# DCN-v2 cross layers: a block transpose on VectorE, x0's rows in eight loads, and one sum on GpSimd

## The chip, the cores and the metric

The kernel runs on one core of a Trainium2 chip. The metric is device time in microseconds (us) of one execution; lower is better. The core has TensorE (matrix multiply, PE in the profile, its weight loads PEld), VectorE (DVE), ScalarE (ACT), GpSimd (POOL) and SyncE (SP, which here only issues transfers). Each engine works through its own list of instructions in order and waits for others on semaphores. A transfer (DMA) is issued by an instruction in some engine's list: SPq and ACTq are the rows of those issues.

## What is computed

Six cross layers over a batch of 4096 rows of 416 features, all in bfloat16:

```python
B, F, D, L = 4096, 26, 16, 6
Din = min(F * D, 1024)            # 416
def reference(x0, ws, bs):        # x0 (B, Din), ws (L, Din, Din), bs (L, Din)
    x = x0
    for l in range(ws.shape[0]):
        x = x0 * (x @ ws[l] + bs[l]) + x
    return x
```

## The kernel before

**Layout.** Layers 0 to 4 keep x transposed: features on partitions, batch along the row. The 416 features are three blocks of 128 (`XM`, index m or k) and a remainder of 32 (`XR`). The batch is two halves s = 0, 1 of 2048 (`SW`), each of four groups g of 512 columns (`CW`). The remainder of a half is folded: partitions 32g to 32g+31 of `XR` hold the 32 remainder features of group g, so that a half is one 128x512 tile. `XRd` is the same with its upper and lower 64 partitions exchanged; the first layer uses it for m = 1 (line 218).

**Loads.** SP issues, in this order: the transposing loads of x0 into `XM[0]` (`load_x0t`, line 75; two groups interleaved with ScalarE's issues, then the rest), after the fifth of them `xrem` (the 32 remainder features of the second half, line 84), three more transposing loads, the weights of layer 1 (line 71), the remainder rows of the weights `WR` (line 90), the weights of layers 2 to 5, x0 by rows `X0rows` in four loads of eight 128-row blocks (line 123), and the last layer's bias `bLr` (line 125). ScalarE issues the weights of layer 0, the biases, the first half's remainder `xrig[:, 0]` in four loads (line 80) and `WR` of layer 0, and then copies that `WR` to two other partition groups (line 108), GpSimd to a third (line 110). An issue waits first for the previous transfer that used the same one of eight transfer semaphores.

**The remainder of x0.** It has to be transposed. `x0_rem(s, tpr)` (line 153) does it on TensorE: four 128x128 transposes of `xrig` into PSUM, then three VectorE copies out of PSUM, one to `XR[0]` and two of 64 partitions, exchanged, to `XRd`. For the first half it stands in the middle of the first six matmul groups of layer 0; for the second half it stands after the first half's remainder matmuls (`mm_rem`), in the other half of the PSUM tile `pr` (line 255). For the second half GpSimd first rearranges `xrem` into `xrig[:, 1]` (line 132).

**Layer 0** (`first_layer`) works on a half as two times 1024 columns (h), for each m a PSUM tile `ph`. PSUM holds four such tiles. `ew_main` evicts a tile: ScalarE adds the bias (line 163), VectorE multiplies by x0 (line 164) and adds x (line 167). `ew_rem` does the same for the folded remainder (lines 171 to 173). Layers 1 to 4 run through the same steps, with `mm_full`, `mm_row` and `mm_rem`.

**The last layer** turns the product round, so that the batch rows come out on partitions: the transposed x is the stationary operand and the weights stream (lines 325, 331, 334; the bias enters by a matmul with ones). x itself is transposed back into `XLrows` by transposing transfers. The 32 blocks of 128 rows are done in four rounds of eight. A block's PSUM result is cast by ScalarE into `t` (line 352), multiplied by `X0rows` on VectorE (line 353), and `XLrows` is added on VectorE (line 342); then the result `o` is stored. A sum is put off by one: `ew` emits the product of a block and then `close_sum` emits the sum of the block before it, with its store. The first rounds handle two blocks in one instruction (832 elements), the last round, from q = 6, eight single blocks u = 0 to 7 (416 elements). Stores are issued by SP, that of the very last block by ScalarE (line 367).

The order of instructions on each engine is made by a scheduler when the program is built; `tc.keep_in_program_order` fixes an instruction's place relative to the others fixed on the same engine. Each tile pool gives out a fixed number of buffers in turn: six `t`, ten `o`, four PSUM tiles.

Of the kernel before, what the change touches and what calls it, by code (L numbers as in the profile page):

```python
# [10 lines left out]
ALU = mybir.AluOpType  # L11
BF16 = mybir.dt.bfloat16
# [4 lines left out]
def kernel(  # L17
# [7 lines left out]
    nc = tc.nc  # L25
    B, D = x0.shape
    L = ws.shape[0]
    P = 128
    NK = 3
    R = D - NK * P  # L30
    assert R == 32 and B == 4096 and D == 416 and L >= 2
    NS = 2
    NG = 4
    CW = 512
    SW = NG * CW
# [4 lines left out]
    big = ctx.enter_context(tc.tile_pool(name="big", bufs=1))  # L40
# [4 lines left out]
    x0_v = x0.rearrange("(bt p) d -> p bt d", p=P)  # L45
    out_v = out.rearrange("(bt p) d -> p bt d", p=P)

    ident = const.tile([P, P], BF16)
# [9 lines left out]
    X0rows = big.tile([P, NBT, D], BF16)  # L58
    XLrows = big.tile([P, NBT, D], BF16)
    scrR = [big.tile([P, 4, P], BF16, name=f"scrR{s}") for s in range(NS)]  # L60
    xrem = big.tile([P, 16, R], BF16)
    xrig = big.tile([P, NS, 4, P], BF16)
    XRd = big.tile([P, NS * CW], BF16)
    XM = [big.tile([P, NK, B], BF16, name=f"XM{i}") for i in range(3)]
    XR = [big.tile([P, NS * CW], BF16, name=f"XR{i}") for i in range(3)]

    def col0(s, g):
        return SW * s + CW * g

    def load_wm(eng, l):  # L70
        eng.dma_start(WM[:, l], ws[l, 0:NK * P, :].rearrange("(k p) n -> p k n", p=P))

    def load_x0t(s, g):
        c0 = col0(s, g)
        nc.sync.dma_start_transpose(out=XM[0][:, :, c0:c0 + CW], in_=x0[c0:c0 + CW, 0:NK * P])

    def load_xrem0():
        with nc.allow_non_contiguous_dma(reason="64B row segments"):
            for i in range(4):
                nc.scalar.dma_start(xrig[:, 0, i, :].rearrange("p (g r) -> p g r", g=NG), x0_v[:, i:16:4, NK * P:D])  # L80

    def load_xrem1():
        with nc.allow_non_contiguous_dma(reason="64B row segments"):
            nc.sync.dma_start(xrem[:], x0_v[:, 16:32, NK * P:D])

    def load_wr0():
        nc.scalar.dma_start(WR[0:R, 0, :], ws[0, NK * P:D, :])
# [17 lines left out]
    for g in range(1, NG):  # L105
        dst, src = WR[32 * g:32 * g + 32, 0, :], WR[0:R, 0, :]
# [4 lines left out]
    for g in range(2, NG):  # L111
        load_x0t(0, g)
    load_x0t(1, 0)
    load_xrem1()
    for g in range(1, NG):
        load_x0t(1, g)
    load_wm(nc.sync, 1)
# [1 line left out]
        load_wr(nc.sync, g, 1, L)  # L119
    for l in range(2, L):  # L120
        load_wm(nc.sync, l)
    for q in range(4):
        nc.sync.dma_start(X0rows[:, 8 * q:8 * q + 8, :], x0_v[:, 8 * q:8 * q + 8, :])
    for g in range(NG):
        nc.sync.dma_start(bLr[32 * g:32 * g + 1, :], bs[LL:LL + 1, :])

    def fill_wd(l0, l1):
        for g in range(NG):
            nc.gpsimd.tensor_copy(WD[32 * g:32 * g + 32, l0:l1, g, :], WR[32 * g:32 * g + 32, l0:l1, NK * P:D])

    fill_wd(0, 1)
    nc.gpsimd.tensor_copy(xrig[:, 1].rearrange("p i (g r) -> p i g r", g=NG), xrem[:].rearrange("p (g i) r -> p i g r", g=NG))
    fill_wd(1, L)

    wps = psum.tile([P, CW], FP32, tag="ps", name="wps")
# [14 lines left out]
        nc.vector.tensor_copy(bM[:], pb[:, 0:NK, 0:L])  # L150
        nc.vector.tensor_copy(bR[:], pb[:, 3, 0:L])

    def x0_rem(s, tpr):
        for i in range(4):
            nc.tensor.transpose(tpr[:, 128 * i:128 * i + 128], xrig[:, s, i, :], ident[:])  # L155
        for dst, src in ((slice(0, P), slice(0, P)), (slice(64, P), slice(0, 64)), (slice(0, 64), slice(64, P))):
            to = XR[0] if dst == src else XRd
            nc.vector.tensor_copy(to[dst, CW * s:CW * s + CW], tpr[src])

    def ew_main(l, s, m, h, pt, cur, nxt, pin=False):  # L160
        c0 = col0(s, 2 * h)
        t = tpool.tile([P, 2 * CW], BF16, name="t")
        nc.scalar.activation(t[:], pt[:].rearrange("p a b -> p (a b)"), ACT.Identity, bias=bM[:, m, l:l + 1], scale=1.0)  # L163
        prod = nc.vector.tensor_tensor(out=t[:], in0=t[:], in1=XM[0][:, m, c0:c0 + 2 * CW], op=ALU.mult)  # L164
        if pin:
            tc.keep_in_program_order(prod)
        nc.vector.tensor_tensor(out=nxt[:, m, c0:c0 + 2 * CW], in0=t[:], in1=cur[:, m, c0:c0 + 2 * CW], op=ALU.add)  # L167
# [38 lines left out]
    def first_layer(s):  # L206
        cur, curR, nxt, nxtR = XM[0], XR[0], XM[1], XR[1]

        def full(pt, m, h, gl, after_row):
            c0 = col0(s, 2 * h + gl)  # L210
            for k in range(NK):
                nc.tensor.matmul(pt[:, gl, :], lhsT=WM[:, 0, k, 128 * m:128 * m + 128], rhs=cur[:, k, c0:c0 + CW],  # L212
                                 start=(k == 0 and not after_row), stop=(k == NK - 1 and after_row))

        def row(pt, m, h, opens):
            for gl in range(2):
                rg = 32 * ((2 * h + gl) ^ (2 if m == 1 else 0))
                src = XRd if m == 1 else curR
                nc.tensor.matmul(pt[:, gl, :], lhsT=WR[rg:rg + 32, 0, 128 * m:128 * m + 128],  # L219
                                 rhs=src[rg:rg + 32, CW * s:CW * s + CW],  # L220
                                 start=opens, stop=not opens, tile_position=(rg, 0))

        def ph(m):
            return psum.tile([P, 2, CW], FP32, tag="ps", name=f"ph{m}")

        pa = [ph(m) for m in range(NK)]
        if s == 0:
            for m in range(NK):
                full(pa[m], m, 0, 0, False)
            tp0 = psum.tile([P, CW], BF16, tag="ps", name="tpr")  # L230
            x0_rem(0, tp0[:])
            for m in range(NK):
                full(pa[m], m, 0, 1, False)
        else:
            for m in range(NK):
                for gl in range(2):
                    full(pa[m], m, 0, gl, False)
        pb = [ph(0)]
        row(pa[0], 0, 0, False)
        row(pb[0], 0, 1, True)  # L240
        row(pa[2], 2, 0, False)
        row(pa[1], 1, 0, False)
        for m in range(NK):
            ew_main(0, s, m, 0, pa[m], cur, nxt)
        for m in range(NK):
            if m:
                pb.append(ph(m))
            for gl in range(2):
                full(pb[m], m, 1, gl, m == 0)
        row(pb[1], 1, 1, False)  # L250
        row(pb[2], 2, 1, False)
        pr = psum.tile([P, 2, CW], FP32, tag="ps", name="pr")
        mm_rem(0, s, pr[:, 0, :], cur, curR)
        if s == 0:
            x0_rem(1, pr[:, 1, :].bitcast(BF16)[:, 0:CW])
        for m in range(NK):
            ew_main(0, s, m, 1, pb[m], cur, nxt, pin=(s == 0))
        ew_rem(0, s, pr[:, 0, :], curR, nxtR)
# [3 lines left out]
    for s in range(NS):  # L262
        first_layer(s)
# [16 lines left out]
    for l in range(1, LL):  # L280
        nxt, nxtR = XM[1 + (l % 2)], XR[1 + (l % 2)]
        feeds_last = (l == LL - 1)
        tiles = [(s, m) for s in range(NS) for m in range(NK)]
# [31 lines left out]
    NQ = len(quads)  # L315
# [7 lines left out]
    def mm_q_full(q, g, py, closes):  # L323
        for k in range(NK):
            nc.tensor.matmul(py[:, 0:D], lhsT=cur[:, k, q_cols(q, g)], rhs=WM[:, l, k, :],  # L325
                             start=((not closes) and k == 0), stop=(closes and k == NK - 1))
# [8 lines left out]
                             rhs=bLr[32 * g:32 * g + 1, :], start=False, stop=(g < done), tile_position=(32 * g, 0))  # L335

    pending = []

    def close_sum():
        while pending:  # L340
            o, t, xl, dst, eng = pending.pop()
            tc.keep_in_program_order(nc.vector.tensor_tensor(out=o, in0=t, in1=xl, op=ALU.add))  # L342
            eng.dma_start(dst, o)

    def ew(q, g0, n, src, eng):
        s, i = quads[q]
        b0 = 16 * s + 4 * g0 + i
        b = slice(b0, b0 + 4 * (n - 1) + 1, 4)
        t = tpool.tile([P, 2 * CW], BF16, name="t")
        o = opool.tile([P, 2, D], BF16, name="o")  # L350
        tv = t[:, 0:n * D].rearrange("p (a d) -> p a d", a=n)
        nc.scalar.copy(tv, src)  # L352
        tc.keep_in_program_order(nc.vector.tensor_tensor(out=tv, in0=tv, in1=X0rows[:, b, :], op=ALU.mult))  # L353
        close_sum()
        pending.append((o[:, 0:n, :], tv, XLrows[:, b, :], out_v[:, b, :], eng))

    PAIRS = [(0, 0), (0, 1), (1, 0), (1, 1), (2, 0), (2, 1), (3, 0), (3, 1)]
# [3 lines left out]
    for q, at, done in rounds:  # L361
        tiles = [psum.tile([P, 2, CW], FP32, tag="ps", name=f"py{n}") for n in range(4)]
        bank = [tiles[n][:, a, :] for n, a in at]

        def close(u, n):
            tl, a = at[u]
            ew(q + u // 4, u % 4, n, tiles[tl][:, a:a + n, 0:D], nc.scalar if q + 2 == NQ and u == 7 else nc.sync)

        for u in range(done):
            mm_q_full(q, u, bank[u], False)  # L370
        mm_q_rem(q, bank[0:4], done)
        close(0, done)
        mm_q_rem(q + 1, bank[4:8], 0)
        for u in range(done, 8):
            mm_q_full(q + u // 4, u % 4, bank[u], True)
            if at is not PAIRS:
                close(u, 1)
            elif u % 2:
                close(u - 1, 2)
    close_sum()  # L380


# [28 lines left out]
```

## Time and profile before

| what | value |
|---|---|
| runs | 130.68, 130.64, 130.82 us (median 130.68) |
| profiled execution | 130.58 us, of which the span of its instructions is 128.8 |
| TensorE busy | 123.6 us (96% of the span), 1691 matmuls |
| VectorE busy | 106.7 us (83%), 195 instructions |
| ScalarE busy | 86.9 us (67%), 99 instructions |
| GpSimd busy | 6.2 us (5%), 18 instructions |
| transfers | 16.37 MB; the 16 transfer engines nearly always busy up to about 39 us |
| TensorE clock granted | full in every slice of the span |

Times in the views are from the start of the span. A timeline row has start, duration, engine, line, operation, output and inputs, shapes and, after x, how many instructions it merges. A row of the groups of instructions has, after the count, the busy time in us and the mean of one in ns, then the idle time just before them and what ended it. A row of the chain of waits has start, duration, engine, tile and line.

### The profile page before, as it was taken

What the parts mean: (1) busy time and instruction counts of PE and PEld (TensorE: products, weight loads), DVE (VectorE), ACT (ScalarE), POOL (GpSimd) and SP (SyncE); (2) the same over time, 40 slices, a digit from 0 to 9 for tenths busy, and PEclk for the clock granted to TensorE, in tenths of its full rate; (3) what the DMA queues carried; (4) which work ended last, traced back from release to release, by engine and by line L of the source; (5) the groups of instructions that cost most, each with busy time, mean ns of one, the idle gap of its engine ahead of it and who ended that gap; (6) DMA issues with size and microseconds to landing.
All of it is one profiled execution on the core that took longest, in us unless ns stands there. A gap on an engine that the chain in (4) does not pass through costs nothing.

```text
span 128.8 us, 3973 instructions
## 1 busy us (share of the span) xinstructions
PE 123.6 (96%) x1691; PEld 55.1 (43%) x1691; DVE 106.7 (83%) x195; ACT 86.9 (67%) x99; POOL 6.2 (5%) x18
## 2 busy tenths in 40 slices
PE   7999999999999999999999999999999999999960
PEld 3343443344545444434444544444444445445420
DVE  0023989999999898989898989898989899898991
ACT  0138873887848667848668848668858896569670
POOL 4004300600000000000000000000000000000000
PEclk9999999999999999999999999999999999999999
DMA  4999999999990000000000000000297999985754
GB/s 95 244 231 207 163 153 264 253 328 333 336 291 9 5 0 8 0 0 5 0 5 0 5 0 5 0 5 0 45 163 169 119 237 191 217 261 186 235 178 138
DMA packets 42102, 16.37 MB, mean 127 GB/s; under 512 B 30906, under 2 KB 42084, under 8 KB 42084
## 3 DMA queue, kind: packets, MB, share of 16 engines
q1 hardware_dynamic: 39368, 15.53, 53.9%
q10 hardware_dynamic: 2716, 0.59, 2.5%
q8 instruction: 13, 0.21, 0.7%
q14 instruction: 5, 0.04, 0.1%
HBM read 6.15 MB, written 3.41 MB: 74 GB/s over the span
## 4 chain that ended last, share of the span: by engine, by line
PE 89%; DVE 6%; issue 2%; ACT 1%; DVEq 0%
PE pt L179 49%; PE ph L212 13%; PE py L325 8%; PE pt L185 5%; PE pr L196 5%; PE wps L139 4%; DVE t L353 4%; DVE o L342 2%; PE pr L191 2%; PE ph L219 1%; PE py L331 1%; PE py L334 1%; ACT t L352 1%; PE tpr L155 0%; PE pr L155 0%
## 5 line engine op out<-in xcount | busy, mean ns | idle before, releaser
L179 PE MATMUL pt<-XM,WM 128*32 128x512 bf16 x1152 | 65.2, 379 | 0.0
L163 ACT ACTIVATE t<-pt,bM 128x1024 bf16<-128x1024 f32 x48 | 49.6, 1115 | 18.5 <-PE pt L185 18.5
L164 DVE TENSOR_TENSOR t<-t,XM 128x1024 bf16<-128x1024 bf16 x60 | 41.4, 690 | 5.2 <-ACT t L163 5.2
L167 DVE TENSOR_TENSOR XM<-t,XM 128x1024 bf16<-128x1024 bf16 x60 | 41.8, 697 | 3.4
L179 PEld LDWEIGHTS <-WM 128*32 128x32 bf16 x1152 | 29.7, 97 | 33.8 <-issue 5.1
L352 ACT CAST t<-py 128x416 bf16<-128x416 f32 (+1 forms) x23 | 14.8, 642 | 4.8 <-PE py L325 2.6
L325 PE MATMUL py<-WM,XM 128*128 128x416 bf16 x96 | 17.7, 340 | 0.0
L212 PE MATMUL ph<-XM,WM 128*128 128x512 bf16 x72 | 16.5, 381 | 0.0
L163 ACT ACTIVATE t<-ph,bM 128x1024 bf16<-128x1024 f32 x12 | 12.5, 1114 | 3.4 <-PE ph L219 3.4
L325 PEld LDWEIGHTS <-XM 128*128 128x128 bf16 x96 | 9.0, 98 | 8.5 <-issue 1.4
L353 DVE TENSOR_TENSOR t<-t,X0rows 128x416 bf16<-128x416 bf16 (+1 forms) x23 | 10.4, 457 | 1.2 <-ACT t L352 1.2
L342 DVE TENSOR_TENSOR o<-t,XLrows 128x416 bf16<-128x416 bf16 (+1 forms) x23 | 10.4, 456 | 0.0
L212 PEld LDWEIGHTS <-WM 128*128 128x128 bf16 x72 | 6.7, 98 | 8.4 <-issue 1.1
L171 ACT ACTIVATE t<-pr,bR 128x512 bf16<-128x512 f32 x10 | 6.4, 685 | 2.7 <-PE pr L196 2.1
L196 PE MATMUL pr<-XM,WM 128*32 128x512 bf16 x120 | 8.2, 379 | 0.0
L185 PE MATMUL pt<-XR,WR 32*128 32x512 bf16 x96 | 7.3, 379 | 0.0
L139 PE MATMUL wps<-const-bfloat16-1.0 128*128 128x512 bf16 (+1 forms) x12 | 4.9, 592 | 0.8 <-PEq L395 0.8
L104 ACT ACT_TABLE_LOAD x1 | 1.3, 1283 | 6.0 <-DMA XM<-in_x_dram 6.0
L173 DVE TENSOR_TENSOR XR<-t,XR 128x512 bf16<-128x512 bf16 x10 | 4.2, 425 | 0.7
L196 PEld LDWEIGHTS <-WM 128*32 128x32 bf16 x120 | 3.2, 97 | 3.0
L150 DVE CAST bM<-pb 128x18 f32<-128x18 bf16 x1 | 0.2, 177 | 5.1 <-PE pb L149 5.1
L172 DVE TENSOR_TENSOR t<-t,XR 128x512 bf16<-128x512 bf16 x10 | 4.2, 420 | 0.0
(38 smaller groups left out, 33.5 us busy)
## 6 DMA issues: line engine op xcount, KB each, us to landing
X0rows<-in_x_dram SPq DMA_DIRECT2D x4, 832.0 KB, 11.5
out_dram<-o SPq DMA_DIRECT2D x9, 208.0 KB, 2.5
WM<-in_ws_dram SPq DMA_DIRECT2D x5, 312.0 KB
out_dram<-o SPq DMA_DIRECT2D x13, 104.0 KB, 1.9
WR<-in_ws_dram SPq DMA_DIRECT2D x4, 130.0 KB, 4.1
WM<-in_ws_dram ACTq DMA_DIRECT2D x1, 312.0 KB
XM<-in_x_dram SPq DMA_TRANSPOSE x8, 4.9
xrig<-in_x_dram ACTq DMA_DIRECT2D x4, 32.0 KB, 4.2
```

The costliest lines, as they stand in the source:

```text
L139: nc.tensor.matmul(wps[:, 0:cols], lhsT=warm[:, 0:P], rhs=warm[:, 0:cols], start=True, stop=True)
L163: nc.scalar.activation(t[:], pt[:].rearrange("p a b -> p (a b)"), ACT.Identity, bias=bM[:, m, l:l + 1], scale=1.0)
L164: prod = nc.vector.tensor_tensor(out=t[:], in0=t[:], in1=XM[0][:, m, c0:c0 + 2 * CW], op=ALU.mult)
L167: nc.vector.tensor_tensor(out=nxt[:, m, c0:c0 + 2 * CW], in0=t[:], in1=cur[:, m, c0:c0 + 2 * CW], op=ALU.add)
L179: nc.tensor.matmul(pts[g // 2][32 * q:32 * q + 32, g % 2, :], lhsT=WM[:, l, k, 128 * m + 32 * q:128 * m + 32 * q + 32], rhs=cur[:, k, c0:c ...
L185: nc.tensor.matmul(pts[g // 2][:, g % 2, :], lhsT=WR[32 * g:32 * g + 32, l, 128 * m:128 * m + 128], rhs=curR[32 * g:32 * g + 32, CW * s:CW ...
L196: nc.tensor.matmul(pr[32 * g:32 * g + 32, :], lhsT=WM[:, l, k, NK * P:D], rhs=cur[:, k, c0:c0 + CW], start=False, stop=(k == NK - 1), tile ...
L212: nc.tensor.matmul(pt[:, gl, :], lhsT=WM[:, 0, k, 128 * m:128 * m + 128], rhs=cur[:, k, c0:c0 + CW], start=(k == 0 and not after_row), sto ...
L325: nc.tensor.matmul(py[:, 0:D], lhsT=cur[:, k, q_cols(q, g)], rhs=WM[:, l, k, :], start=((not closes) and k == 0), stop=(closes and k == NK ...
L342: tc.keep_in_program_order(nc.vector.tensor_tensor(out=o, in0=t, in1=xl, op=ALU.add))
L352: nc.scalar.copy(tv, src)
L353: tc.keep_in_program_order(nc.vector.tensor_tensor(out=tv, in0=tv, in1=X0rows[:, b, :], op=ALU.mult))
```

## The change

Three things are changed.

First, the remainder of the second half is no longer transposed by TensorE. `xrem` is loaded in another layout, partition p holding the sixteen batch rows 16p to 16p+15 of the half, by ScalarE and not by SP. The load is made to wait for a one-column memset of `xrem` that VectorE executes after the first half's copies. Then VectorE transposes `xrem` in blocks of 32x32 directly into `XR[0]`, and makes the two exchanged copies to `XRd` from `XR[0]`, in SBUF. The four TensorE transposes, the three copies from PSUM and GpSimd's rearrangement of `xrem` go; `xrig` keeps the first half alone. VectorE's instructions of both halves are now fixed in program order.

Second, `X0rows` is loaded in eight transfers of four blocks for four of eight.

Third, in the last round the sum of block u = 3 is made by GpSimd, fixed in program order, and its store is issued by ScalarE. `close_sum` has one sum less to do.

```diff
-    xrig = big.tile([P, NS, 4, P], BF16)
+    xrig = big.tile([P, 4, P], BF16)
...
+    def pin(ins):
+        tc.keep_in_program_order(ins)
...
     def load_xrem1():
+        pin(nc.vector.memset(xrem[:, 0, 0:1], 0.0))
         with nc.allow_non_contiguous_dma(reason="64B row segments"):
-            nc.sync.dma_start(xrem[:], x0_v[:, 16:32, NK * P:D])
+            pin(nc.scalar.dma_start(xrem[:], x0[SW:2 * SW, NK * P:D].rearrange("(p t) r -> p t r", p=P)))
...
     load_x0t(1, 0)
-    load_xrem1()
     for g in range(1, NG):
...
-    for q in range(4):
-        nc.sync.dma_start(X0rows[:, 8 * q:8 * q + 8, :], x0_v[:, 8 * q:8 * q + 8, :])
+    for q in range(8):
+        nc.sync.dma_start(X0rows[:, 4 * q:4 * q + 4, :], x0_v[:, 4 * q:4 * q + 4, :])
...
     fill_wd(0, 1)
-    nc.gpsimd.tensor_copy(xrig[:, 1].rearrange("p i (g r) -> p i g r", g=NG), xrem[:].rearrange("p (g i) r -> p i g r", g=NG))
     fill_wd(1, L)
...
-    def x0_rem(s, tpr):
+    def x0_rem0(tpr):
         for i in range(4):
-            nc.tensor.transpose(tpr[:, 128 * i:128 * i + 128], xrig[:, s, i, :], ident[:])
+            nc.tensor.transpose(tpr[:, 128 * i:128 * i + 128], xrig[:, i, :], ident[:])
         for dst, src in ((slice(0, P), slice(0, P)), (slice(64, P), slice(0, 64)), (slice(0, 64), slice(64, P))):
             to = XR[0] if dst == src else XRd
-            nc.vector.tensor_copy(to[dst, CW * s:CW * s + CW], tpr[src])
+            pin(nc.vector.tensor_copy(to[dst, 0:CW], tpr[src]))
+        load_xrem1()
+
+    def x0_rem1():
+        pin(nc.vector.transpose(XR[0][:, CW:2 * CW].rearrange("p (j t) -> p t j", t=16), xrem[:]))
+        for dst, src in ((slice(64, P), slice(0, 64)), (slice(0, 64), slice(64, P))):
+            pin(nc.vector.tensor_copy(XRd[dst, CW:2 * CW], XR[0][src, CW:2 * CW]))
...
         if s == 0:
-            x0_rem(1, pr[:, 1, :].bitcast(BF16)[:, 0:CW])
+            x0_rem1()
...
     pending = []
+    late = []
...
-    def ew(q, g0, n, src, eng):
+    def ew(q, g0, n, src, eng, on_pool=False):
...
         close_sum()
+        if on_pool:
+            tc.keep_in_program_order(nc.gpsimd.tensor_tensor(out=o[:, 0:n, :], in0=tv, in1=XLrows[:, b, :], op=ALU.add))
+            late.append((out_v[:, b, :], o[:, 0:n, :]))
+            return
         pending.append((o[:, 0:n, :], tv, XLrows[:, b, :], out_v[:, b, :], eng))
...
-            ew(q + u // 4, u % 4, n, tiles[tl][:, a:a + n, 0:D], nc.scalar if q + 2 == NQ and u == 7 else nc.sync)
+            ew(q + u // 4, u % 4, n, tiles[tl][:, a:a + n, 0:D], nc.scalar if q + 2 == NQ and u == 7 else nc.sync,
+               q + 2 == NQ and u == 3)
...
+    for dst, o in late:
+        nc.scalar.dma_start(dst, o)
     close_sum()
```

In the order that the scheduler builds, the load of `xrem` stands on ScalarE right after the two `WR` copies and before the first eviction; VectorE's block transpose stands where the three copies from PSUM stood, after the first half's first three pairs of product and sum; and ScalarE's store of u = 3 stands between the casts of u = 5 and u = 6, with a wait for GpSimd, although the source has it after the loop.

More of the change, by code (lines that the diff above doesn't have):

```diff
@@ L79, in load_xrem0 @@
             for i in range(4):
-                nc.scalar.dma_start(xrig[:, 0, i, :].rearrange("p (g r) -> p g r", g=NG), x0_v[:, i:16:4, NK * P:D])
+                nc.scalar.dma_start(xrig[:, i, :].rearrange("p (g r) -> p g r", g=NG), x0_v[:, i:16:4, NK * P:D])
     def load_xrem1():
+        pin(nc.vector.memset(xrem[:, 0, 0:1], 0.0))
         with nc.allow_non_contiguous_dma(reason="64B row segments"):
-            nc.sync.dma_start(xrem[:], x0_v[:, 16:32, NK * P:D])
+            pin(nc.scalar.dma_start(xrem[:], x0[SW:2 * SW, NK * P:D].rearrange("(p t) r -> p t r", p=P)))
     def load_wr0():
@@ L230, in first_layer @@
             tp0 = psum.tile([P, CW], BF16, tag="ps", name="tpr")
-            x0_rem(0, tp0[:])
+            x0_rem0(tp0[:])
             for m in range(NK):
```

## The prediction

> **What bounds the kernel now.** I read the chain of waits first, with the page's summary of it, in order of time:
>
> ```profile
> PE 89%; DVE 6%; issue 2%; ACT 1%; DVEq 0%
> 16.06 0.65 PE pr L196 x12
> 16.71 0.33 PE pr L155 x4
> 17.04 3.88 PE ph L212 x18
> ...
> 115.45 0.19 PE py L334 x2
> 115.65 0.02 issue
> 115.67 0.86 ACT t L352
> ...
> 125.24 0.37 DVE t L353
> 125.62 0.29 DVE o L342
> 125.90 0.28 DVEq L406
> ```
>
> TensorE runs without a gap from 0.77 to 115.65 us, so what it no longer executes there is time saved; the four transposes of line 155 for the second half are such a piece, 0.33 us. From 115.67 the chain goes over to ScalarE and VectorE. To see which of them ends the last round I read the timeline around 123 us, VectorE and then ScalarE:
>
> ```profile
> 122.97 0.37 DVE L353 TENSOR_TENSOR t<-t,X0rows 128x416 bf16<-128x416 bf16 x1
> 123.25 0.37 DVE L342 TENSOR_TENSOR o<-t,XLrows 128x416 bf16<-128x416 bf16 x1
> ...
> 125.24 0.37 DVE L353 TENSOR_TENSOR t<-t,X0rows 128x416 bf16<-128x416 bf16 x1
> 125.53 0.66 DVE L342 TENSOR_TENSOR o<-t,XLrows 128x416 bf16<-128x416 bf16 x2
> 126.22 0.37 ACTq L343 DMA_DIRECT2D out_dram<-o  x1
> ```
>
> ```profile
> 123.39 1.03 ACT L352 CAST t<-py 128x416 bf16<-128x416 f32 x2
> 124.44 0.51 ACT L352 CAST t<-py 128x416 bf16<-128x416 f32 x1
> ```
>
> Call the blocks of the last round u0 to u7. VectorE starts an instruction every 0.285 us (122.97 to 123.25), two per block, 0.57; ScalarE's casts come every 0.525 us back to back, u5's at 123.39 (to 123.90), u6's at 123.92, u7's at 124.44 (to 124.95). The last product starts at 125.24, 0.29 after its cast. Both engines are thus nearly full here: VectorE is the slower by 0.04 per block, and ScalarE has no hole to put anything in. After the last product come 0.95 us (125.24 to 126.19, two sums) and the last store.
>
> **The change, part by part.** Sums are made against the profiled execution, 130.58 us (span 128.8 and 1.78 around it); the median of the three runs is 0.10 above it.
>
> *Removed from TensorE:* four transposes, 0.33 us of the chain (0.40 busy by their row). I take -0.33. It holds if what follows does not come late:
>
> - VectorE's block transpose with its two copies stands where the three PSUM copies stood (17.08 to 18.40). No row shows such a transpose. Lower bound: one 128x512 pass, 0.42 (lines 172, 173). Upper: sixteen blocks at the price of the small 128x18 cast, 0.177 each, 2.8 us. The data decide the start: the load of xrem took 4.6 us to land on SP's queue, and the four xrig loads on ScalarE's, issued from 1.90, were there at 8.33, 6.4 us. Issued at about 10.8 it lands between 15.4 and 17.2; VectorE is free at 16.31 (line 167 at 15.62 took 0.98 beside GpSimd's xrig copy, which goes, and 0.69 elsewhere). With two copies of 0.42 it ends between 17.6 and 20.9; as one pass is the nearest row, I take 18. TensorE wants the result with line 219 at 20.93 - 0.33 = 20.60, so only the slow end shows, by 0.3. Queued behind it on VectorE are the products of that half (line 164), whose cover is the 1.9 us between line 173's end at 31.55 and TensorE's use of it at 33.47.
> - The xrem load now stands on ScalarE between the two WR copies (end 10.76) and the first eviction (11.09), and waits for a memset on VectorE, which is idle after 9.99. Its issue costs 0.37 to 0.66 (the xrig issues), so the first eviction ends by 10.78 + 0.66 + 1.11 = 12.55. TensorE wants that PSUM tile for the seventh of eighteen matmuls, 11.42 + 6 x 0.222 = 12.75. Hidden by 0.2 us; price nothing, bound 0.1.
> - SP loses one issue (0.58) ahead of three transposing loads, which so start earlier by more than TensorE's 0.33.
>
> *Eight loads of X0rows for four:* four issues more on SP, between 23.28 and 31.1, with the bias rows behind them. Their first readers are at 107.43 and about 105. Covered by some 70 us, nothing; bare, up to 4 x 1.96 = 7.8.
>
> *The sum of u3.* VectorE loses one instruction, 0.285. Alone, the last product could start right after its cast, 124.97 for 125.24: -0.27. But in the built order of ScalarE's instructions the store of u3 stands between the casts of u5 and u6, and waits for GpSimd. That a waiting DMA issue holds what stands behind it on ScalarE the trace of before shows:
>
> ```profile
> 5.64 0.34 ACTq L87 DMA_DIRECT2D WR<-in_ws_dram  x1
> 6.00 1.28 ACT L104 ACT_TABLE_LOAD   x1 [6.00 <-DMA XM<-in_x_dram]
> ```
>
> The table load needs no data, yet it starts when the issue ahead of it, which waited for an earlier transfer, is through. So the casts of u6 and u7 wait for the sum on GpSimd. Its length T decides, and no row has a two-input operation there; the nearest are
>
> ```profile
> L132 POOL COPY xrig<-xrem 128x512 bf16<-128x512 bf16 x1 | 1.1, 1057 | 3.7 <-DMA xrem<-in_x_dram 3.7
> L96 POOL MEMSET WD<- 128x768 bf16 x1 | 0.7, 737 | 0.0
> L110 POOL COPY WR<-WR 32x416 bf16<-32x416 bf16 x1 | 0.5, 524 | 7.6 <-DMA WR<-in_ws_dram 7.6
> L95 POOL MEMSET ones<- 128x128 bf16 x1 | 0.2, 204 | 0.0
> ```
>
> The two memsets give (737 - 204)/640 = 0.83 ns per element; the 416-element copy fits that with 0.18 us fixed. Lower bound of T: that copy, 0.52. Upper: two passes at the rate of the 512-element copy, 2 x 1.06 x 416/512 = 1.72. I take two passes at 0.83 ns, 0.69 + 0.18 = 0.87, and add what the copy beside a busy VectorE was longer than its line (1.06 - 0.60 = 0.46, for 416 elements 0.37), as VectorE is busy here too: T = 1.24.
>
> [...]
>
> Now the times, in those of before. The product of u3 ends at 122.97 + 0.37 = 123.34; GpSimd starts some 0.11 later (line 110 started 0.12 after ScalarE's copy that waited for the same load): 123.45. It ends at 123.45 + T; a hand-off (0.03 to 0.05) and the issue (0.37), with the start of the next cast, add 0.44. So u6's cast starts at 123.89 + T, u7's ends 1.04 later, its product starts 0.03 after, and 0.95 later the last sum is done: 125.91 + T, for 126.19. This part costs T - 0.28: at 1.24, +0.96; at the bounds +0.24 and +1.44.
>
> **Sum:** -0.33 + 0.96 = +0.63: 131.21 on the profiled execution, 131.31 on the median. I say 131.25. At the bounds of T it is 130.59 and 131.79 on the median.
>
> **Rivals.**
> 1. *GpSimd's sum is short,* T of 0.52 to 0.87. For it: the plain copy of as many elements. Against: one input fewer, 32 partitions, no VectorE contending. 130.6 to 130.9.
> 2. *The store doesn't hold the casts* (the other side: faster). If ScalarE can cast u6 while the store waits for GpSimd, u6 stays at 123.92 and both gains stand: -0.33 - 0.27 = -0.60, 130.1. It decides if u6's cast starts before GpSimd's end. For it: compute and issue are shown as separate rows, ACT and ACTq. Against: the table load above, and the built order.
> 3. *The start loses its gain:* the block transpose costs over 2.5 us, or xrem lands late, and TensorE waits at line 219. Then the 0.33 is gone or reversed: 131.6 to 132. Against: 2.6 us between my 18 and 20.60.
> 4. *The change doesn't do what it says* would be a sum still on VectorE; the built order has it on GpSimd, so it gets no chance.
>
> **How the numbers follow.** The measurement tells about 0.2% (0.26 us) from no change, that is, outside 130.42 to 130.94. Forecast 0.70 (own range 130.95 to 131.8), rival 1 0.14, rival 2 0.11, rival 3 0.05. Slower is forecast and rival 3, 0.75; same is rival 1, 0.14; faster rival 2, 0.11. The range, 130.4 to 131.9, takes in both bounds of T and rival 1, and leaves out rival 2 and the far end of rival 3. The time is the forecast's.
>
> **What would show it.** In the profile after: the four line-155 transposes of the second half are missing from the chain and TensorE reaches the last round about 0.33 earlier; one GpSimd two-input row of about 1.2 us; a hole in ScalarE between the sixth and seventh casts of the last round, ended by GpSimd, of about T - 0.45 + 0.37; VectorE idle before the last two products; the chain's end passing through GpSimd and ScalarE's store. A GpSimd row under 0.6 us, or casts that go on at 0.525, makes the forecast wrong; so does a TensorE gap before line 220 or 227 of the new file's first stage.

## The result, and the profile after

| kernel | runs | median us | ratio to before (95% interval) |
|---|---|---|---|
| before, beside it | 6 | 130.66 | |
| changed | 6 | 131.80 | 1.0099 (1.0087 to 1.0111) |

The change makes the kernel slower by 1.14 us (131.80 - 130.66). The forecast was 131.25 with a range of 130.4 to 131.9: the direction was right and 131.80 lies inside the range, near its upper end, but the loss is nearly twice the +0.63 of the sum. The profiled execution of the changed kernel took 132.27 us (span 130.5), which is 0.47 above the median of its runs; so not all that it shows belongs to a typical run, as will be seen.

The chain of waits of the changed kernel, in order of time, with the page's line of its shares by engine on top. Columns as before.

```profile
PE 63%; DVE 17%; DMA 10%; issue 3%; ACTq 2%; POOLq 1%; ACT 1%; DVEq 0%
10.22 6.68 DMA xrem<-in_x_dram
...
16.93 2.37 DVE XR L164
...
33.24 0.35 DVE XR L181
33.59 0.04 issue
33.63 0.40 PE pr L199 x4
...
115.80 0.19 PE py L342 x2
...
123.31 0.38 DVE t L362
123.69 0.03 POOLq L365
...
123.79 1.02 POOLq L422
```

Before, TensorE made up 89% of the chain, without a gap up to 115.65. Now the chain stays on TensorE only from 33.63 on, and what stands ahead of it is the load of xrem, which lands at 16.91, the block transpose (line 164) and VectorE's work up to the second half's remainder of layer 1 (line 181). TensorE's last bias matmuls are at 115.80 for 115.45, so in this execution the front is 0.35 us late and not 0.33 early. The rest is made in the last round, and there the chain passes through GpSimd. The timeline of the changed kernel from the cast of u5 on:

```profile
123.74 0.51 ACT L361 CAST t<-py 128x416 bf16<-128x416 f32 x1
123.82 0.97 POOL L365 TENSOR_TENSOR o<-t,XLrows 128x416 bf16<-128x416 bf16 x1 [98.70 <-DMA out_dram<-o]
123.89 1.15 DVE L362 TENSOR_TENSOR t<-t,X0rows 128x416 bf16<-128x416 bf16 x1
...
124.83 0.38 ACTq L395 DMA_DIRECT2D out_dram<-o  x1
125.24 0.36 DVE L351 TENSOR_TENSOR o<-t,XLrows 128x416 bf16<-128x416 bf16 x1
125.59 0.91 ACT L361 CAST t<-py 128x416 bf16<-128x416 f32 x2 [1.35 <-DVE t L362]
...
126.70 0.37 DVE L362 TENSOR_TENSOR t<-t,X0rows 128x416 bf16<-128x416 bf16 x1
126.99 0.65 DVE L351 TENSOR_TENSOR o<-t,XLrows 128x416 bf16<-128x416 bf16 x2
```

Two things are to be seen. GpSimd's sum takes 0.97 us, ScalarE's store is issued when it has ended (123.82 + 0.97 = 124.79, issue at 124.83), and the casts of u6 and u7 come only after that, at 125.59, though the cast of u5 ended at 124.25 (123.74 + 0.51). (The bracket there names a product of VectorE as what ended the wait; the buffer that the cast of u6 needs was free since the sum of u0, at about 122.8, so it was the issue in front of it.) And the product of u4 on VectorE, which has nothing to do with GpSimd's data, takes 1.15 us for 0.37: it begins 0.07 after GpSimd and ends 0.25 after it (123.89 + 1.15 = 125.04). The last sum is done at 127.64 (126.99 + 0.65) for 126.19 before: +1.45, of which 0.35 came from the front.

### The profile page after: what moved, and what is told of

Read it like the earlier page. It is cut to its first block, busy times and chain, and to the rows that moved or that the text cites. A ratio compares the mean times of both kernels' runs of the same rounds, so it can differ in the third digit from the quotient of the medians.

```text
span 130.5 us, 3971 instructions
## 1 busy us (share of the span) xinstructions
PE 123.5 (95%) x1687; PEld 55.1 (42%) x1687; DVE 108.7 (83%) x195; ACT 86.6 (66%) x99; POOL 5.9 (5%) x18
## 4 chain that ended last, share of the span: by engine, by line
PE 63%; DVE 17%; DMA 10%; issue 3%; ACTq 2%; POOLq 1%; ACT 1%; DVEq 0%
PE pt L187 45%; PE py L333 8%; DMA xrem<-in_x_dram 5%; PE pt L193 5%; DVE t L172 4%; DMA xrig<-in_x_dram 4%; DVE XM L175 4%; PE pr L204 3%; DVE t L362 3%; DVE o L351 2%; DVE XR L164 2%; PE pr L199 1%; DMA out_dram<-o 1%; PE py L339 1%; ACTq L83 1%
## 5 line engine op out<-in xcount | busy, mean ns | idle before, releaser
L362 DVE TENSOR_TENSOR t<-t,X0rows 128x416 bf16<-128x416 bf16 (+1 forms) x23 | 11.1, 489 | 1.7 <-ACT t L361 1.7
L365 POOL TENSOR_TENSOR o<-t,XLrows 128x416 bf16<-128x416 bf16 x1 | 1.0, 974 | 98.7 <-DMA out_dram<-o 98.7
```

## The experiments

Every kernel was timed in five rounds beside the kernel before on the same chip, except the one for single costs. The kernel before stood at 130.50, 130.56, 130.55 and 130.66 us (medians of 17 to 24 runs) in the four sets. Theory A is that most of the loss is made in the last round.

| experiment | median us | ratio to before (95% interval) |
|---|---|---|
| third part alone (GpSimd's sum, ScalarE's store) | 131.36 | 1.0065 (1.0051 to 1.0078) |
| first part alone (block transpose) | 130.53 | 1.0002 (0.9990 to 1.0014) |
| second part alone (eight loads) | 130.77 | 1.0024 (1.0015 to 1.0034) |
| third part, store by SP | 130.94 | 1.0032 (1.0021 to 1.0044) |
| eight loads and four tiny ones | 130.58 | 1.0001 (0.9992 to 1.0011) |
| block transpose written contiguously | 130.65 | 0.9998 (0.9982 to 1.0014) |
| no transposes for the second half | 130.62 | 0.9994 (0.9980 to 1.0008) |
| contiguous transpose, xrem loaded by SP | 130.51 | 0.9999 (0.9980 to 1.0018) |
| changed kernel, store by SP, four tiny loads | 131.10 | 1.0030 (1.0018 to 1.0042) |
| changed kernel, no GpSimd sum, four tiny loads | 130.54 | 0.9995 (0.9982 to 1.0009) |

### Each part alone

The third part alone is the last piece of the diff (`on_pool`, `late`) on the kernel before.

> The kernel before with the third part alone (sum of u3 on GpSimd, its store on ScalarE). Theory A, most of the loss is made in the last round, by ScalarE held behind the store and by VectorE slowed beside GpSimd's sum: +1.1 us, 131.6 to 132.0. Rival B, the loss is made at the start by VectorE's block transpose: at most +0.3, 130.5 to 131.0.

Measured: 131.36 against 130.50, +0.86. That is theory A's direction, though less than the +1.1 expected; rival B is out. The +1.1 had been read from the changed kernel's one profile (1.45 - 0.35), in which the cast of u6 starts 0.28 us later behind the store's issue than in this kernel's profile (last section); the missing 0.25 is about that.

The first part alone is the diff without its second and third pieces.

> The kernel before with the first part alone (block transpose on VectorE, load of xrem on ScalarE). Theory A: the transpose of 2.35 us uses up VectorE's slack and TensorE waits once at the second half's remainder of layer 1, which eats the 0.33 us of the four transposes and a little more: 130.7 to 131.0. Rival B: it carries most of the loss, over 131.3. The prediction's view: 130.3.

Measured: 130.53 against 130.50. No change that can be told: neither the gain of the prediction nor a loss. In its profile the transpose also took 2.36 us, but xrem landed in time (the transpose began at 16.18, not 16.93), and TensorE did not wait at the second half's remainder of layer 1 (it began at 33.19, the block before it having ended on VectorE at 32.72). The wait in the changed kernel's profile is thus that of an execution in which xrem came 0.75 later; it explains why that execution was slow, not the loss in the median. The first half's remainder matmuls ended at 16.65 and the last layer began at 103.43: 86.78 us for 87.00 before (16.71 to 103.71). So the four transposes are worth 0.22 us on TensorE, not 0.33. This repeats: the profiles of five other kernels here that keep the transposes have 87.00 or 87.01, those of three more without them, in which TensorE waits nowhere in between, 86.78. The eighteen matmuls behind them took 3.88 us of the chain before and take 4.00 here (16.65 to 20.65).

The second part alone:

```diff
-    for q in range(4):
-        nc.sync.dma_start(X0rows[:, 8 * q:8 * q + 8, :], x0_v[:, 8 * q:8 * q + 8, :])
+    for q in range(8):
+        nc.sync.dma_start(X0rows[:, 4 * q:4 * q + 4, :], x0_v[:, 4 * q:4 * q + 4, :])
```

> The kernel before with the eight loads of X0rows alone. All theories: no change, within 0.1 us of 130.66. A rival for the rest of the loss, the order of the loads at the start, would show here as more than 0.2 us.

Measured: 130.77 against 130.50, +0.27, with an interval that lies wholly above 1. The theories missed this one. Only the rival named in the expectation, the order of the loads at the start, fits the number, and the next section shows that it is not that. The three parts give 0.86 + 0.03 + 0.27 = 1.16, the 1.14 of the whole.

### Why eight loads cost

The loads themselves were done long before they were needed: in the changed kernel's profile the last of the eight was issued at 30.9 and took 9.0 us to land, and the first product that reads them starts at 107.8, 68 us later. What they shift is the count of transfers: each transfer signals the next of eight semaphores in turn, and four more transfers move the kernel's last store from semaphore 7 to semaphore 3. At the very end SP waits for all of them, in the order that the build gives it: 3 and 2, 4 and 1, 5 and 0, 6, 7. The waits of SP at the end, in total, number and longest: of the kernel before, then of the kernel with eight loads, then of the changed kernel.

```profile
SPq L406 <- DMA out_dram<-o: 1.4, 4, 0.5
```

```profile
SPq L406 <- DMA out_dram<-o: 1.7, 1, 1.7
```

```profile
SPq L422 <- DMA out_dram<-o: 1.7, 1, 1.7
```

Before, SP met the stores one by one, and the last one to land was the last one asked. With eight loads the last one to land is asked first: one wait of 1.7 us, and the four other waits follow it. In the kernel with eight loads they can be seen in the list of line 406, first SP's seven semaphore instructions, of which the first five are these waits, with the first and the last start; then the instructions of which the first stands behind the five:

```profile
L406 SPq EVENT_SEMAPHORE  x7: 17/28/28, 128.1 to 129.1; - x7
...
L406 SPq DRAIN  x3: 7/7/7, 128.4 to 128.7; - x3
```

The first wait ends when the last store has landed, at 128.1, and SP is through all five at 128.4, 0.3 later. To test this, four tiny loads into an unused tile were added, behind the bias rows, which bring the last store back to semaphore 7:

```diff
+    extra = const.tile([P, D], BF16)
+    for g in range(4):
+        nc.sync.dma_start(extra[32 * g:32 * g + 1, :], bs[0:1, :])
```

> The eight loads of X0rows and, behind the bias rows, four more tiny loads into an unused tile, which move the last store from transfer semaphore 3 back to 7, the one that SP asks last at the end. Theory (the order in which SP asks the semaphores at the end costs the eight loads' 0.27 us): as the kernel before, 130.4 to 130.6, and SP's wait at the end is again split into four. Rival (the additional issues themselves cost): 130.8 or more.

Measured: 130.58 against 130.56, and the wait is in pieces again:

```profile
SPq L409 <- DMA out_dram<-o: 1.4, 3, 0.5
```

Four transfers more made the kernel with eight loads faster, back to the time before. So neither the additional issues nor the eight loads at the start cost anything that can be told; the semaphore of the last store does.

### The hold, and VectorE beside GpSimd's sum

The third part with another issuer of the store:

```diff
     for dst, o in late:
-        nc.scalar.dma_start(dst, o)
+        nc.sync.dma_start(dst, o)
```

> As the third part alone, but the store of u3 is issued by SP, so that ScalarE isn't held. If both the hold and VectorE's slowing cost (A): the product of u4 still takes about 1.15 us beside GpSimd and VectorE ends the chain about 0.5 later than before, 131.1 to 131.3. If the hold is all: the sum saved on VectorE shows, 130.4. If VectorE's slowing is all: as with the store on ScalarE, about 131.75.

Measured: 130.94 against 130.50, +0.44, half of the +0.86 with ScalarE's store and near the +0.5 expected if both causes hold. In the profile of this kernel the timeline shows the casts free and VectorE not:

```profile
121.69 3.14 ACT L353 CAST t<-py 128x416 bf16<-128x416 f32 x6
...
123.36 0.97 POOL L357 TENSOR_TENSOR o<-t,XLrows 128x416 bf16<-128x416 bf16 x1 [97.72 <-DMA out_dram<-o]
123.42 1.43 DVE L354 TENSOR_TENSOR t<-t,X0rows 128x416 bf16<-128x416 bf16 x2
```

The casts run through at their pace (six in 3.14 us), but two products still take 1.43 us, where two starts 0.285 apart take 0.66. VectorE lost about 0.77 (1.43 - 0.66) and was spared 0.285: +0.49, near the measured +0.44. With ScalarE's store, the casts of u6 and u7 are late as well, and the two delays overlap: +0.42 more, not the whole of the hold. So both of theory A's causes hold, each for about half.

Is GpSimd slowed, or VectorE, or both? The costs by themselves were measured in the idle time at the start of the kernel before: VectorE transposes a tile twice, with the strided output of the change (line 106) and with a contiguous one (line 107), then GpSimd adds 416 elements while VectorE stands idle (line 108).

```diff
...
+    pn(nc.vector.transpose(mb[:].rearrange("p (j t) -> p t j", t=16), ma[:]))
+    pn(nc.vector.transpose(mc[:].rearrange("p (t j) -> p t j", t=16), ma[:]))
+    pn(nc.gpsimd.tensor_tensor(out=md[:], in0=mb[:, 0:D], in1=mc[:, 0:D], op=ALU.add))
...
```

> Disputed costs by themselves, in the idle time at the start of the kernel before: VectorE's block transpose of a 128x512 tile with the strided output of the change and with a contiguous one, and GpSimd's sum of 416 elements with VectorE idle. If the output's stride is the cost: about 2.35 us strided and 0.5 to 0.8 contiguous; if the block transpose is slow by itself: both near 2.35. If VectorE's contention falls on VectorE alone, GpSimd's sum takes about 0.97 here too; if GpSimd was slowed beside it, 0.6 to 0.8.

The groups of instructions of that kernel, VectorE's:

```profile
L106 DVE STREAM_TRANSPOSE mb<-ma 128x512 bf16<-128x512 bf16 x1 | 2.3, 2318 | 0.0
...
L107 DVE STREAM_TRANSPOSE mc<-ma 128x512 bf16<-128x512 bf16 x1 | 0.9, 859 | 0.0
```

and GpSimd's:

```profile
L108 POOL TENSOR_TENSOR md<-mb,mc 128x416 bf16<-128x416 bf16 x1 | 1.0, 971 | 2.3 <-DVE mc L107 2.3
```

GpSimd's sum takes 0.97 alone and 0.97 beside VectorE: it loses nothing, and VectorE alone pays. What VectorE pays rests on the kernels with the sum in the last round; a second sum and four products, put in to run side by side here too, did not meet (the products began at 6.13, the sum, again 0.97 long, at 10.56). The transpose is slow because of the stride of its output, 32 bytes from one element to the next: 2.32 us for 0.86.

### What the four transposes are worth

The first part with a contiguous transpose:

```diff
-        pin(nc.vector.transpose(XR[0][:, CW:2 * CW].rearrange("p (j t) -> p t j", t=16), xrem[:]))
+        pin(nc.vector.transpose(xtr[:], xrem[:]))
+        pin(nc.vector.tensor_copy(XR[0][:, CW:2 * CW].rearrange("p (j t) -> p j t", t=16), xtr[:].rearrange("p t j -> p j t")))
```

> The first part alone, with the block transpose written contiguously to another tile and the columns put in order by the copy to XR[0]. If the stride is the cost: the transpose takes 0.5 to 0.8, the block ends about 1 us earlier on VectorE, TensorE doesn't wait any more where xrem lands late, and the 0.28 to 0.33 us of the four transposes show in each run: 130.15 to 130.25, closer together than with the strided output. If the transpose is slow by itself: 130.5 or more, as spread as before.

Measured: the transpose took 0.71 us and the copy 0.59, VectorE was through 1.02 us sooner than in the changed kernel's profile (18.94 for 19.96, with xrem landing equally late) and TensorE did not wait at the second remainder. But the time did not move by an amount that can be told: 130.65 against 130.56, with runs from 130.37 to 130.91, where 130.15 to 130.25 was expected. The stride is the cost of the transpose, but without it the median shows no gain either. The next kernel takes the four transposes out and puts almost nothing in their place: `x0_rem(1)` copies the first half's result, so that the second half's own remainder of x0 is left out.

```diff
-        for i in range(4):
-            nc.tensor.transpose(tpr[:, 128 * i:128 * i + 128], xrig[:, s, i, :], ident[:])
+        if s == 0:
+            for i in range(4):
+                nc.tensor.transpose(tpr[:, 128 * i:128 * i + 128], xrig[:, s, i, :], ident[:])
...
-            nc.vector.tensor_copy(to[dst, CW * s:CW * s + CW], tpr[src])
+            nc.vector.tensor_copy(to[dst, CW * s:CW * s + CW], tpr[src] if s == 0 else XR[0][src, 0:CW])
```

> The kernel before without the second half's four transposes: the second half's remainder is copied from the first half's instead (the second half's own remainder of x0 is left out). It shows what the four transposes are worth on TensorE when nothing takes their place. If the 0.33 us of the chain were all saved: 130.2. If the weight loads behind the transposes hid a part, as the profiles with the block transpose show (TensorE 0.22 earlier): 130.3. If saving at the start is given back later: 130.5.

Measured: 130.62 against 130.55, from 130.24 to 130.90. The interval leaves out a gain of 0.33 (a ratio of 0.9975) but not one of 0.22 (0.9983). In the profile TensorE has the 0.22: from the end of the first half's remainder to the last layer it takes 86.78 (17.09 to 103.87). But that execution was late before it came there:

```profile
2.18 6.84 DMA XM<-in_x_dram
...
9.06 2.10 PE ph L213 x9
```

TensorE waited for the second transposing load of x0, which landed at 9.02, and the second nine matmuls of layer 0 began at 9.06 for 8.63 before. Neither the loads nor TensorE's instructions ahead of that point differ between the two kernels, so the missing transposes did not make this wait. In the six kernels here that keep the transposes these matmuls began between 8.54 and 8.84, from execution to execution: a spread larger than the gain.

Last, the candidate to beat both kernels: the contiguous transpose with xrem loaded by SP after the fifth transposing load, as before the change, and no memset.

```diff
-        pin(nc.vector.memset(xrem[:, 0, 0:1], 0.0))
...
-            pin(nc.scalar.dma_start(xrem[:], x0[SW:2 * SW, NK * P:D].rearrange("(p t) r -> p t r", p=P)))
+            nc.sync.dma_start(xrem[:], x0[SW:2 * SW, NK * P:D].rearrange("(p t) r -> p t r", p=P))
...
```

> The contiguous block transpose, with the load of xrem back on SP in its old place, without memset (candidate to beat both kernels). If the late landing of xrem (16.9 us against 14.9) keeps the first part from showing TensorE's gain: 130.25 to 130.35, with a narrow spread. If not: 130.5, as the contiguous transpose with ScalarE's load.

Measured: 130.51 against 130.55, from 130.30 to 131.52. It is faster than the changed kernel and no faster than the one before. Its chain of waits shows what took the gain in that execution:

```profile
10.94 6.49 DMA XM<-in_x_dram
17.43 0.04 issue
17.48 2.32 PE ph L221 x10
```

TensorE began the second half's first matmuls at 16.58, came to the fourth, the first to need the next transposing load of x0, at about 17.24 (three at 0.22), and stood until that load had landed at 17.43. Before, the four transposes put that point at 17.70 (17.04 + 0.66). But this wait is this kernel's: xrem stands ahead of that load on SP again, and the load was issued at 10.94. Where ScalarE issues xrem it was issued at 10.24 to 10.56, and the profiles of those kernels do not have the wait. So there is not one cause. Of the seven profiles without the four transposes, four have TensorE's gain whole (86.78), one lost it to this load, and two lost some or all of it to VectorE's late block at the second remainder of layer 1 (the changed kernel's, and that of the last kernel below). Over the medians the gain stays unseen: a gain of 0.33 lies outside the interval of each of the five kernels that have neither these transposes nor GpSimd's sum; one of 0.22 lies outside that of the first part alone (0.9990 to 1.0014) and inside those of the other four. What takes it there is not shown, as one execution of each was profiled.

### The causes added up

The changed kernel with the store of u3 on SP and the four tiny loads:

> The changed kernel with two of the found costs taken out: the store of u3 issued by SP, and four tiny loads more, so that the last store is again on the semaphore asked last. If the causes add up (hold 0.42, order of the semaphores 0.27): 131.8 - 0.7 = 131.1, that is 0.45 above the kernel before, what GpSimd's sum costs through VectorE. If something else of the change costs: 131.3 or more.

Measured: 131.10 against 130.66, +0.44, as with GpSimd's sum and SP's store alone. And the changed kernel with the four tiny loads and the sum on VectorE again:

> The changed kernel with the sum of u3 on VectorE again and its store on SP, and the four tiny loads: what is left is the block transpose and the eight loads. If the causes add up: no change against the kernel before, 0.998 to 1.002. If something else costs: over 1.002.

Measured: 130.54 against 130.66, no change that can be told. So the 1.14 us consist, to 0.01, of 0.44 for VectorE held beside GpSimd's sum, 0.42 for ScalarE's casts held behind the store, and 0.27 for the last store's semaphore. The first part costs and brings nothing that the medians tell.

## Why the forecast had the direction right and the size wrong

In the sum's own terms, -0.33 became 0, the eight loads' 0 became +0.27, and GpSimd's +0.96 became +0.86: +1.13 for +0.63. That 131.80 lies inside the range is luck: its upper end stands for T = 1.72, and T was 0.97.

- **The four transposes, -0.33.** Wrong; this step failed. The chain of one execution showed TensorE without a gap, and I took its instructions for time. They are 0.22 on TensorE (86.78 for 87.00), and the medians show nothing of it, with nothing in their place either (0.9994, 0.9980 to 1.0008). The step "it holds if what follows does not come late" covered what follows and not what stands ahead: the loads at the start moved TensorE's second nine matmuls between 8.54 and 9.06 from profile to profile. Whether that, or the waits seen in three profiles, takes the gain in a typical run stays open.
- **The block transpose.** I took the end of VectorE's block for 18; it was 19.18 in the profile of the first part alone and 19.93 in the changed kernel's. I chose the price of one pass, and the row was 2.35 us, near the upper bound of 2.8. My estimate had no price for the stride of its output: the contiguous one took 0.70 to 0.86 us for 128x512, the strided one 2.32 to 2.36. I also placed TensorE's first need of the delay at line 219; it showed up 13 us later, at the second remainder of layer 1, behind VectorE's queue, which I had given 1.9 us of cover. That cover was too short by some 0.4 in one profile (the block ended at 33.59 for 31.55 before), by 0.15 in that of the last kernel (TensorE's four matmuls there took 0.37 for 0.22), and enough in the two others with the strided transpose.
- **The load of xrem on ScalarE.** The transposing load that had stood behind xrem on SP did start earlier, at 10.45 for 10.95, and xrem landed at 16.91, inside the forecast 15.4 to 17.2. That the issue is hidden on ScalarE was right, for more than the given reason: its issue stood at 10.22 beside ScalarE's running copies, and the first eviction began at 11.27, right behind TensorE.
- **The eight loads, nothing.** Wrong; the second step that failed. I named 70 us of cover for the data, and 0.27 us came from where the last store stands among eight semaphores. The zero counted the loads alone, not what they shift behind them.
- **GpSimd's sum, T - 0.28 = +0.96.** Nearly right in size (measured +0.86), with two errors that cancel, which is luck. T was 0.97, not 1.24: I had added 0.37 to GpSimd for its sharing with VectorE. The price of running side by side falls on VectorE: 1.15 for 0.37 on the product of u4, which the formula had at nothing. With 0.97 the formula gives +0.69; what is left is 0.17. In the profile of the third part alone a part of that is to be seen: the cast of u7 ended at 125.72, and its product began only at 125.93, behind the product of u6 and the sum of u5, 0.21 for the formula's 0.03. VectorE's two instructions per block set the pace again there.
- **The hold of ScalarE.** Right: the casts of u6 and u7 waited for GpSimd, and rival 2 did not come about.

What holds VectorE's product beside GpSimd's sum is not shown. The rows show its size alone: the product that began 0.07 after GpSimd ended 0.25 after it, GpSimd lost nothing (0.97 both times), and VectorE lost 0.77 of that 0.97.

## What to carry to other kernels

A sum given to GpSimd can take its time from VectorE as well: here, beside two products, 0.285 us were saved and 0.77 lost, before any wait. The store placed between two casts on ScalarE held them until its data were there (in the changed kernel's profile 1.34 us from the end of u5's cast to u6's, and 0.42 us of the median); give it to an engine that has nothing else to do. Where a chain shows an engine without gaps in a stretch in which the transfer engines are nearly always busy too, take some work out and see whether the time follows before counting it as a gain.

## What was not expected of the hardware

- The order in which the end of the program asks its semaphores is worth 0.27 us (0.2%): the last store should signal the one that is asked last. Beside the eight loads, four useless transfers of 832 bytes were faster than none (130.58 us for 130.77).
- A block transpose on VectorE whose output elements lie 32 bytes apart took 2.32 to 2.36 us, and 0.70 to 0.86 with a contiguous output; the strided copy that puts the columns in order took 0.59, so that both together (1.30) are cheaper than the one.
- In the changed kernel's profile the cast of u6 began 0.38 us after the store's issue had ended (124.83 + 0.38 = 125.21, cast at 125.59); in the kernel with the third part alone it was 0.10 us (issue from 124.34 to 124.71, cast at 124.81). Why was not settled.
